# Complex-decay attention with an MLP on one core: weight loads without gates, the log's clip as a job of its own, rstd on two engines, and another order of all jobs

## Chip, cores and metric

The kernel runs on one core of a Trainium2 chip. The metric is the time of one execution on the device in microseconds (us); a lower one is better. The kernel before takes 197.36 us, the median of three runs (196.34 to 197.73). All times are of the fast state unless a run says otherwise.

## The reference, cut to what matters

```python
# q, k, v, a_re, a_im: (4, 8, 768, 48) float32
mag = np.sqrt(a_re**2 + a_im**2)
scale = np.minimum(mag, 0.999) / (mag + 1e-06)      # a complex decay, clipped to 0.999
for t in range(768):                                # S_re, S_im: 48 x 48 for each head
    S_re, S_im = ar*S_re - ai*S_im + k_t v_t^T,  ar*S_im + ai*S_re
    y[t] = q_t @ S_re
x = y with heads side by side                       # (4, 768, 384)
xn = (x - mean) / sqrt(var + 1e-6) * g_ln
out = x + relu(xn @ w_ch1) @ w_ch2                  # 384 -> 1536 -> 384
```

The kernel computes the recurrence in blocks of 128 steps ("tiles", 24 of them), two to a "pair" (12 pairs). For each pair the logarithm and the angle of the decay are summed along time by matmuls, queries and keys are scaled by exponentials and rotated by cosines and sines, and the tile becomes a masked product. The MLP follows per pair.

## The kernel before: the parts that matter here

Every piece of work is a named job, and a long string gives the order of all jobs. Each engine runs its own jobs **strictly in that order**; the letter behind the name is the engine (P TensorE, A ScalarE, V VectorE, G GpSimd, S the loading queue), the digit a PSUM bank.

```python
GATES = (("k", 0, 1), ("aim", 1, 0))
PLAN = """
are.0.1:S tab.log.0:A ln.0.1:A iv.0.1:A aim.0.1:S ... gate.1:G q.0.0:S q.0.1:S warm.0:P1 warm.1:P1
... gate.0:G tab.trig.0:A ... r.2.0:G ... G.0:V1
atm.1:V6 atm.0:V2 y.1:P0 y.0:P6 ... x.0:A6 l.2.0:V dec.2.0:P2 wl.1:G
..."""
```

The weight loads are issued by GpSimd, each behind a tiny copy (the "gate") that waits for an input, so that they don't start before it has landed:

```python
for i, (nm, P, c) in enumerate(GATES):
    g.add(f"gate.{i}", ... nc.gpsimd.tensor_copy(out=probe, in_=...), needs=[f"{nm}.{P}.{c}"], ...)
g.add("wl.0", lambda: nc.gpsimd.dma_start(out=w1b, ...), needs=["gate.0"])
g.add("wl.1", lambda: nc.gpsimd.dma_start(out=w2b, ...), needs=["gate.1"])
```

The log of the decay and its clip are one job of two VectorE instructions:

```python
def f_l(S_=S_):
    nc.vector.scalar_tensor_tensor(out=S_("l"), in0=S_("r2"), scalar=0.5, in1=S_("w"), ...)   # the log
    nc.vector.tensor_scalar(out=S_("l"), in0=S_("l"), scalar1=LNCAP, scalar2=LNEPS,
                            op0=ALU.min, op1=ALU.add)                                        # the clip
```

Jobs named below: `r` is the product of imaginary part and inverse, `ke` and `qe` scale keys and queries, `ks` and `qs` rotate them, `kT`/`ksT` and `qT`/`qsT` are their transposes and the copies out of PSUM, `am`/`atm` the tile's product and its masking, `y` the tile's result, `dec` the matmuls that sum the clipped log, `e` and `en` the exponentials, `wp`/`wc` the folding of the layer norm into w1, `ot` the output's last sum, `bn` and `rstd` the layer norm's statistics, and `warm` a matmul without a result that is meant to keep TensorE's clock up.

Of the kernel before, what the change touches and what calls it, by code (L numbers as in the profile page):

```python
# [33 lines left out]
GATES = (("k", 0, 1), ("aim", 1, 0))  # L34
# [5 lines left out]
are.0.1:S tab.log.0:A ln.0.1:A iv.0.1:A aim.0.1:S are.0.0:S pad.ks.1:G one:G ue:G car0.1:G cmean:G pick:G  # L40
ident:G uth:V zdec:G r.0.1:G aim.0.0:S are.1.0:S ln.0.0:A iv.0.0:A r.0.0:V gln:S aim.1.0:S k.0.0:S are.3.0:S
k.0.1:S r2.0.1:A u.0.1:A pad.ks.2:G l.0.1:V ln.1.0:A r2.0.0:G gate.1:G q.0.0:S q.0.1:S warm.0:P1 warm.1:P1
warm.2:P1 warm.3:P1 warm.4:P1 warm.5:P1 warm.6:P1 warm.7:P1 warm.8:P1 warm.9:P1 warm.10:P1 warm.11:P1
warm.12:P1 warm.13:P1 warm.14:P1 warm.15:P1 warm.16:P1 warm.17:P1 warm.18:P1 warm.19:P1 warm.20:P1
warm.21:P1 warm.22:P1 warm.23:P1 warm.24:P1 warm.25:P1 warm.26:P1 warm.27:P1 warm.28:P1 warm.29:P1
warm.30:P1 warm.31:P1 warm.32:P1 warm.33:P1 dec.0.1:P0 u.0.0:A iv.1.0:A l.0.0:V r.1.0:V car0.0:G en.0.1:A0
e.0.1:A0 q.1.0:S r2.1.0:V pad.qs.0:G gate.0:G tab.trig.0:A th.0.1:A warm.34:P2 warm.35:P2 warm.36:P2
warm.37:P2 warm.38:P2 warm.39:P2 warm.40:P2 warm.41:P2 warm.42:P2 warm.43:P2 warm.44:P2 warm.45:P2
warm.46:P2 warm.47:P2 warm.48:P2 warm.49:P2 warm.50:P2 warm.51:P2 warm.52:P2 ph.0.1:P1 are.2.0:S vf.0.0:S
vf.0.1:S aim.2.0:S th.0.0:A ph.0.0:P0 ke.0.1.0:G abs.0.0:V0 abs.0.1:A1 car.0.1:A1 pad.ks.0:G sin.0.1:A1  # L50
ks.0.1.1:V car.0.0:V0 th.1.0:A warm.53:P4 warm.54:P4 warm.55:P4 warm.56:P4 warm.57:P4 warm.58:P4 warm.59:P4
warm.60:P4 warm.61:P4 ph.1.0:P2 k.1.1:S qe.0.1.0:V cos.0.1:A qs.0.1.0:V cos.0.0:A dec.0.0:P1 sin.0.0:A0
aim.3.0:S vf.1.1:S k.1.0:S abs.1.0:V2 car.1.0:V2 vf.1.0:S q.1.1:S ks.0.1.0:G pad.qs.1:G mask:G tab.log.1:A
en.0.0:A1 e.0.0:A1 qs.0.1.1:V ke.0.0.0:V qe.0.0.0:V ks.0.0.0:V ks.0.0.1:V warm.62:P5 warm.63:P5 warm.64:P5
warm.65:P5 warm.66:P5 warm.67:P5 warm.68:P5 warm.69:P5 warm.70:P5 warm.71:P5 warm.72:P5 warm.73:P5
warm.74:P5 warm.75:P5 warm.76:P5 warm.77:P5 warm.78:P5 warm.79:P5 warm.80:P5 warm.81:P5 warm.82:P5 kT.1:P4
k.2.0:S wl.0:G qs.0.0.1:V u.1.0:A ln.2.0:A qs.0.0.0:V dps.0:P5 k.2.1:S iv.2.0:A l.1.0:V kT.0:P6 qT.1:P7
tab.trig.1:A cos.1.0:A v.0:A ksT.0:V6 r.2.0:G ksT.1:V4 decc.0:V5 wgc:V qsT.1:V7 qT.0:P0 gm.0:P1 dec.1.0:P4
am.1:P6 th.2.0:A sin.1.0:A2 tab.log.2:A e.1.0:A4 r2.2.0:G u.2.0:A pad.qs.2:G qsT.0:V0 am.0:P2 G.0:V1
atm.1:V6 atm.0:V2 y.1:P0 y.0:P6 ln.3.0:A iv.3.0:A wp.2:P7 qe.1.0.0:G x.0:A6 l.2.0:V dec.2.0:P2 wl.1:G  # L60
en.1.0:A4 wp.0:P6 e.2.0:A2 x.1:A0 wc.2.0:V7 wc.2.2:V7 en.2.0:A2 are.4.0:S xtr.0:P0 wc.2.1:V7 dps.1:P7
xtr.1:P4 r.3.0:G xT.0:A0 wp.1:P5 decc.1:A7 ph.2.0:P2 wc.0.0:V6 wc.0.1:V6 bn.0:V wc.0.2:V6 r2.3.0:A xT.1:A4
wc.1.2:V5 wc.1.1:V5 wc.1.0:V5 ke.1.0.0:G ke.1.0.1:G ks.1.0.0:G v.1:G qe.1.0.1:G mm1.0.2.1:P6 gm.1:P1 G.1:V1
mm1.0.2.0:P6 relu.0.2:V6 u.3.0:A aim.4.0:S ks.1.0.1:V qs.1.0.1:V qs.1.0.0:V bn.1:V rstd.0:G abs.2.0:A2
tab.trig.2:A th.3.0:A cos.2.0:A mm1.0.0.1:P4 mm1.0.1.1:P0 mm1.0.0.0:P4 relu.0.0:V4 sin.2.0:A2 k.3.0:S
q.2.1:S mm1.0.1.0:P0 ph.3.0:P6 l.3.0:V relu.0.1:A0 kT.3:P2 gm.2:P3 vf.2.0:S q.2.0:S k.3.1:S kT.2:P0 qT.2:P1
ksT.2:V0 qsT.2:V1 mm2.0.0:P4 mm2.0.1:P4 mm2.0.2:P4 sin.3.0:A6 am.2:P0 abs.3.0:A6 G.2:A3 ksT.3:A2 ke.2.0.0:G
gm.3:P3 qT.3:P5 ke.2.0.1:V ks.2.0.0:V tab.log.3:A ln.4.0:A iv.4.0:A ks.2.0.1:G r.4.0:G atm.2:V0 mm2.1.0:P2
mm2.1.1:P2 qsT.3:V5 vf.2.1:S aim.6.0:S am.3:P0 mm2.1.2:P2 car.3.0:A6 G.3:V3 q.3.1:S q.4.1:S ot.0:V4 kT.5:P3
atm.3:V0 tab.trig.3:A th.4.0:A qe.2.0.1:G qe.2.0.0:G y.2:P5 q.3.0:S are.6.0:S vf.3.1:S st.0:S y.3:P4 x.2:A5  # L70
x.3:A4 kT.4:P6 xtr.2:P7 ot.1:V2 bn.2:V xT.2:V7 xtr.3:P2 xT.3:V2 ksT.4:V6 dec.3.0:P0 mm1.1.0.1:P4
mm1.1.0.0:P4 r2.4.0:A mm1.1.1.1:P6 qs.2.0.1:V qs.2.0.0:V qT.5:P2 mm1.1.1.0:P6 ksT.5:V3 bn.3:V qT.4:P3
tab.log.4:A en.3.0:A0 v.2:A e.3.0:A0 relu.1.1:A6 ph.4.0:P0 relu.1.0:V4 vf.3.0:S gm.4:P4 ke.3.0.1:G qsT.4:V3
am.4:P6 qsT.5:V2 mm2.2.0:P5 am.5:P2 mm2.2.1:P5 tab.trig.4:A cos.3.0:A G.4:A4 rstd.1:G ke.3.0.0:G qe.3.0.1:G
are.5.0:S aim.5.0:S abs.4.0:V0 sin.4.0:A0 car.4.0:A0 atm.4:V6 mm1.1.2.0:P6 dps.3:P4 mm1.1.2.1:P6 tab.log.5:A
u.4.0:A atm.5:V2 qe.3.0.0:G ks.3.0.1:G ks.3.0.0:V qs.3.0.1:V relu.1.2:V6 qs.3.0.0:V y.5:P0 y.4:P1 l.4.0:V
mm2.3.0:P2 x.5:A0 kT.7:P3 mm2.3.1:P2 x.4:A1 xtr.4:P0 mm2.2.2:P5 xtr.5:P1 ln.5.0:A k.4.0:S iv.5.0:A decc.3:A4
ln.6.0:A q.4.0:S k.5.1:S v.3:G ksT.7:V3 dec.4.0:P6 xT.5:V1 xT.4:A0 mm2.3.2:P2 e.4.0:A6 en.4.0:A6 iv.6.0:A
bn.4:V mm1.2.1.1:P0 ot.2:V5 r.5.0:G qsT.7:S r.6.0:G r2.5.0:V mm1.2.1.0:P0 gm.6:P3 qe.4.0.1:V bn.5:V rstd.2:G
ke.4.0.0:G relu.2.1:A0 u.5.0:A mm1.2.0.1:P4 mm1.2.0.0:P4 tab.trig.5:A th.5.0:A mm1.2.2.1:P6 qe.4.0.0:G  # L80
am.7:P0 mm1.2.2.0:P6 ot.3:V2 qsT.6:S ksT.6:S k.5.0:S vf.4.1:S th.6.0:A relu.2.2:A6 vf.4.0:S st.2:S cos.4.0:A
G.6:V3 k.4.1:S q.5.1:S st.1:S gm.7:P3 dps.4:P2 relu.2.0:V4 mm2.5.0:P4 atm.7:V0 l.5.0:V am.6:P0 atm.6:V0
are.8.0:S y.7:P5 mm2.5.1:P4 q.5.0:S ph.5.0:P6 aim.7.0:S mm2.4.0:P0 y.6:P1 x.7:A5 xtr.7:P5 mm2.5.2:P4
r2.6.0:V bn.7:V ke.4.0.1:G v.4:V x.6:V1 xtr.6:P1 sin.5.0:A6 abs.5.0:A6 xT.7:A5 cos.5.0:A decc.4:A2
mm2.4.1:P0 mm2.4.2:P0 are.7.0:S k.6.1:S G.7:V3 ot.5:V4 tab.log.6:A u.6.0:A xT.6:V1 qs.4.0.0:V mm1.3.0.0:P6
dec.5.0:P4 ks.4.0.1:V mm1.3.1.1:P2 ks.4.0.0:V gm.8:P1 mm1.3.0.1:P6 mm1.3.1.0:P2 qs.4.0.1:V ot.4:V0 e.5.0:A4
qe.5.0.0:G kT.9:P0 en.5.0:A4 relu.3.0:A6 kT.8:P4 st.4:S l.6.0:V ln.8.0:A ksT.8:A4 G.8:A1 bn.6:V st.3:S
k.6.0:S qsT.9:S relu.3.1:V2 qe.5.0.1:V qs.5.0.0:V rstd.3:G q.6.1:S aim.8.0:S st.5:S mm1.3.2.0:P6 qT.8:P5
mm1.3.2.1:P6 ln.7.0:A gm.9:P1 relu.3.2:A6 vf.5.0:S mm2.7.0:P4 dec.6.0:P2 qs.5.0.1:G qsT.8:V5 mm2.7.1:P4
iv.7.0:A G.9:V1 ksT.9:V0 ke.5.0.0:V en.6.0:A2 am.8:P6 e.6.0:A2 r.7.0:V vf.5.1:S ph.6.0:P0 mm2.7.2:P4  # L90
qT.10:P5 am.9:P2 vf.6.1:S r2.7.0:A iv.8.0:A ke.5.0.1:V atm.8:V6 ks.5.0.0:G ks.5.0.1:G u.7.0:A y.8:P6 x.8:A6
tab.trig.6:A sin.6.0:A0 r.8.0:G ke.6.0.0:G qT.11:P7 qsT.10:V5 atm.9:V2 qsT.11:V7 mm2.6.0:P5 mm2.6.1:P5
y.9:P6 abs.6.0:A0 car.6.0:A0 kT.10:P7 bn.8:V x.9:V6 ksT.10:V7 xtr.8:P2 kT.11:P3 xtr.9:P6 mm2.6.2:P5 xT.9:A6
xT.8:V2 ksT.11:V3 am.10:P0 vf.6.0:S th.7.0:A mm1.4.1.0:P6 am.11:P2 th.8.0:A ke.6.0.1:G v.5:G mm1.4.1.1:P6
ot.6:V5 oa.7:A4 k.8.1:S are.9.0:S mm1.4.0.0:P4 mm1.4.0.1:P4 atm.10:V0 gm.10:P0 relu.4.1:A6 l.7.0:V
ks.6.0.1:V ph.7.0:P6 y.10:P1 cos.6.0:A atm.11:V2 G.10:V0 y.11:P0 relu.4.0:A4 mm2.9.0:P2 mm1.4.2.1:P4 x.10:V1
x.11:V0 r2.8.0:A mm1.4.2.0:P4 mm2.8.0:P3 dec.7.0:P0 mm2.8.1:P3 mm2.9.1:P2 ks.6.0.0:G car.7.0:A6 sin.7.0:A6
tab.log.7:A ln.9.0:A q.6.0:S q.8.0:S bn.9:V bn.10:V abs.7.0:A6 e.7.0:A0 qe.6.0.1:G qe.6.0.0:G rstd.4:G
ot.7:G v.6:G relu.4.2:V4 mm2.8.2:P3 xtr.10:P4 bn.11:V qs.6.0.0:V en.7.0:A0 qs.6.0.1:V gm.12:P5 dps.6:P6
# [102 lines left out]
def kernel(  # L202
# [60 lines left out]
    def eng(name):  # L263
        return g.ops[name].eng
# [506 lines left out]
```

## Time and profile before

| | before |
|---|---|
| median time, span of the profiled run | 197.36 us, 196.2 us |
| busy: TensorE, VectorE, ScalarE, GpSimd | 178.8, 160.1, 164.1, 107.8 us |
| first matmul of w1 begins at | 39.68 us |
| its TensorE jobs ahead, so *lost in the start* | 11.5 us, 28.2 us |
| *holes* from there to the last matmul | 6.7 us |
| *end*, from the last matmul on | 3.7 us |
| TensorE's granted clock at half, up to the first w1 matmul | 13.7 us |
| full-size logs and clips over their shortest times (0.95 and 0.355 us), in all | 1.1 + 6.7 us |

The three losses in italics, with some 157.7 us of useful matmuls, make the span; the prediction shows how they are worked out. They come from one profiled execution of each kernel, here one of 198.14 us, 0.8 us above the median; differences of about 1 us between two such traces are not firm. The two stretches around the start, with the columns that the prediction explains (length, busy PE, PEld, DVE, ACT, POOL with counts, granted clock, DMA share, GB/s), show what the start costs:

```profile
20.00:30.00 10.00, 6.45 (x92) 5.17 (x92) 9.76 (x19) 9.88 (x12) 5.71 (x5) 0.78 1.03 207
30.00:40.00 10.00, 8.51 (x54) 4.15 (x53) 9.02 (x14) 6.22 (x13) 6.81 (x5) 0.54 1.19 180
```

The clock falls to 0.78 and 0.54 of full, so the busy time of TensorE there is partly half-speed work. The VectorE timeline of pair 2 and the GpSimd timeline of the same moments (start us, length us, engine, line, operation, tiles) show the slow clip:

```profile
30.27 0.95 DVE L449 SCALAR_TENSOR_TENSOR l<-r,w 128x768 f16<-128x768 f16 x1
31.25 1.85 DVE L451 TENSOR_SCALAR l<-l 128x768 f16<-128x768 f16 x1
```

```profile
30.36 2.52 POOL L280 TENSOR_TENSOR r<-aim,are 128x768 f16<-128x768 f32 x1 [0.50 <-ACT are L433]
```

The clip that takes 0.36 us alone got through only when GpSimd's product ended (at 32.88 us). The log before it, begun just ahead of the product, took its 0.95 us.

### The profile page before, as it was taken

The page shows a single profiled execution, that of the slowest core. Times are in us where ns is not written, and L with a number is a line of the kernel's source. Part 1 is how long each engine was busy: PE and PEld are TensorE (multiplying, and loading weights), DVE is VectorE, ACT ScalarE, POOL GpSimd, SP SyncE. Part 2 cuts the span into 40 slices and gives each one's busy share as a digit, 9 for nine tenths or more (in the row PEclk, how much of TensorE's full clock was granted, in tenths as well). Part 3 has the DMA queues.
Part 4 walks back from the last instruction along what each step waited for, and adds up shares of the span by engine and source line. Part 5 has one row for each costly group of instructions (what it writes and reads, how often), then busy time and mean ns, then how long its engine had stood idle before and what let it go on. Part 6 is the DMA issues. An engine that isn't in the chain of part 4 may idle for free.

```text
span 196.2 us, 5114 instructions
## 1 busy us (share of the span) xinstructions
PE 178.8 (91%) x2031; PEld 135.7 (69%) x2032; DVE 160.1 (82%) x268; ACT 164.1 (84%) x226; POOL 107.8 (55%) x127
## 2 busy tenths in 40 slices
PE   4987566999999999999999997999999999998992
PEld 3775443486787777587887785787877868776771
DVE  1449999899999999999998799799969969935702
ACT  4799994989899999999999999897979998565160
POOL 8535558515839359135968699315891376530230
PEclk9999965599999999999999999999999999999999
DMA  5999999999899399899799999999998999994222
GB/s 138 250 220 233 170 233 173 184 242 217 187 250 222 70 172 245 226 230 238 148 226 205 223 163 280 188 212 253 184 222 155 156 203 147 238 197 130 104 84 82
DMA packets 132936, 37.76 MB, mean 192 GB/s; under 512 B 127920, under 2 KB 132528, under 8 KB 132912
## 3 DMA queue, kind: packets, MB, share of 16 engines
q1 hardware_dynamic: 130960, 35.07, 85.3%
q0 software_dynamic: 1952, 2.36, 7.4%
q8 instruction: 16, 0.26, 0.5%
q14 instruction: 8, 0.07, 0.1%
HBM read 28.31 MB, written 4.72 MB: 168 GB/s over the span
## 4 chain that ended last, share of the span: by engine, by line
PE 50%; DVE 20%; ACT 10%; DMA 8%; SPq 5%; issue 4%; POOL 2%; DVEq 0%; POOLq 0%
PE banks L705 16%; PE banks L684 15%; DVE atm L280 5%; DMA are<-in_a_re_dram 4%; SPq L566 3%; PE banks L584 3%; DVE l L449 3%; PE banks L459 3%; DVE h L697 2%; DVE l L451 2%; PE banks L561 2%; DMA q<-in_q_dram 2%; DMA out_dram<-ot 2%; ACT L739 2%; PE banks L655 2%
## 5 line engine op out<-in xcount | busy, mean ns | idle before, releaser
L705 PE MATMUL banks<-w2b,h 128*128 128x384 bf16 x288 | 55.5, 326 | 1.2 <-DVE atm L280 1.1
L684 PE MATMUL banks<-xT,w1b 128*128 128x256 bf16 x432 | 52.2, 272 | 0.4 <-ACT xT L275 0.4
L684 PEld LDWEIGHTS <-w1b 128*128 128x128 bf16 x432 | 41.3, 98 | 7.0 <-issue 1.0
L705 PEld LDWEIGHTS <-h 128*128 128x128 bf16 x288 | 26.2, 98 | 14.9 <-issue 1.6
L280 DVE TENSOR_TENSOR atm<-banks,mask 128x1024 bf16<-128x1024 f32 x24 | 28.9, 1217 | 4.1 <-PE banks L584 4.0
L695 ACT ACTIVATE h<-banks 128x1024 bf16<-128x1024 f32 x27 | 27.0, 1022 | 5.2 <-PE banks L684 5.0
L739 ACT ACT_TABLE_LOAD x20 | 25.7, 1283 | 1.1 <-PEq L755 0.8
L280 POOL TENSOR_TENSOR qe<-q,e 128x384 bf16<-128x384 f32 x16 | 15.8, 996 | 17.3 <-ACT e L463 12.4
L280 POOL TENSOR_TENSOR ks<-ke,trig 128x768 bf16<-128x768 bf16 (+1 forms) x11 | 17.9, 1634 | 12.0 <-DVE ke L280 7.4
L280 POOL TENSOR_TENSOR r<-aim,are 128x768 f16<-128x768 f32 (+1 forms) x9 | 16.5, 1836 | 11.0 <-ACT are L433 11.0
L280 POOL TENSOR_TENSOR ke<-k,en 128x384 bf16<-128x384 f32 x17 | 17.2, 1017 | 8.1 <-ACT en L463 8.1
L719 DVE SCALAR_TENSOR_TENSOR ot<-banks,rstd,x 128x384 f32<-128x384 f32 x20 | 12.0, 610 | 8.7 <-PE banks L705 6.0
L584 PE MATMUL banks<-qsT,ksT 128*128 128x128 bf16 x192 | 15.3, 227 | 1.2 <-DVE qsT L277 1.2
L584 PEld LDWEIGHTS <-ksT 128*128 128x128 bf16 x192 | 12.9, 102 | 3.9 <-issue 2.3
L734 PE MATMUL banks<-u_e 128*128 128x256 f16 x83 | 12.5, 318 | 2.8 <-POOL u_e L312 2.8
L634 PE MATMUL banks<-v,atm 128*128 128x48 bf16 x192 | 12.2, 186 | 1.5 <-DVE atm L280 1.4
L449 DVE SCALAR_TENSOR_TENSOR l<-r,w 128x768 f16<-128x768 f16 (+1 forms) x13 | 12.9, 990 | 0.9 <-ACT r L445 0.8
L634 PEld LDWEIGHTS <-atm 128*128 128x128 bf16 x192 | 10.8, 97 | 3.7 <-DVE atm L280 2.8
L647 DVE BATCH_NORM_STATS2 stats<-x 128x6 f32<-128x384 bf16 x24 | 13.2, 548 | 0.3 <-ACT x L275 0.3
L280 DVE TENSOR_TENSOR qs<-qe,trig 128x768 bf16<-128x768 bf16 (+1 forms) x21 | 12.1, 597 | 1.1 <-POOL qe L280 0.8
L734 PEld LDWEIGHTS <-u_e 128*128 128x128 f16 x83 | 9.4, 113 | 5.0 <-POOL u_e L312 2.4
L477 PE MATMUL banks<-th,u_th 128*128 128x384 f16 (+1 forms) x52 | 12.1, 320 | 0.7 <-ACT th L467 0.7
(91 smaller groups left out, 376.1 us busy)
## 6 DMA issues: line engine op xcount, KB each, us to landing
k<-in_k_dram SPq DMA_DIRECT2D x24, 192.0 KB, 4.2
q<-in_q_dram SPq DMA_DIRECT2D x24, 192.0 KB, 4.1
vf<-in_v_dram SPq DMA_DIRECT2D x24, 192.0 KB, 4.3
out_dram<-ot SPq DMA_DIRECT2D x24, 192.0 KB, 3.2
are<-in_a_re_dram SPq DMA_DIRECT2D x11, 384.0 KB, 4.7
aim<-in_a_im_dram SPq DMA_DIRECT2D x11, 384.0 KB, 5.5
w1b<-in_moe_w_ch_dram POOLq DMA_DIRECT2D x1, 1152.0 KB, 10.1
w2b<-in_moe_w_ch_dram POOLq DMA_DIRECT2D x1, 1152.0 KB, 11.8
```

The costliest lines, as they stand in the source:

```text
L280: {"DVE": nc.vector, "POOL": nc.gpsimd}[eng(name)].tensor_tensor(**kw)
L449: nc.vector.scalar_tensor_tensor(out=S_("l"), in0=S_("r2"), scalar=0.5, in1=S_("w"), op0=ALU.mult, op1=ALU.add)
L477: nc.tensor.matmul(heads(ps[:, c]), lhsT=u_th[:, c, j], rhs=step(T("th", P), j), start=False, stop=(j == R - 1))
L584: nc.tensor.matmul(ps[:, h], lhsT=T("ksT", n)[:, h], rhs=T("qsT", n)[:, h], start=True, stop=True)
L634: nc.tensor.matmul(ps[:, h], lhsT=T("atm", n)[:, h], rhs=T("v", P)[:, c, h], start=True, stop=nfirst)
L647: nc.vector.bn_stats(out=T("stats", n), in_=T("x", n))
L684: nc.tensor.matmul(ps[:, jj], lhsT=w1b[:, dc, ts(gi * JG + jj, C)], rhs=T("xT", P)[:, dc].rearrange("p c t -> p (c t)"), start=(dc == 0), ...
L695: act(out=dst, in_=src, func=AF.Relu)
L705: nc.tensor.matmul(bank(f"o.{n}")[:, 0:DM], lhsT=T("h", P)[:, j, ts(c, C)], rhs=w2b[:, j], start=(j == 0), stop=(j == NJ - 1))
L719: nc.vector.scalar_tensor_tensor(out=T("ot", n), in0=bank(f"o.{n}")[:, 0:DM], scalar=T("rstd", P)[:, ds(c, 1)], in1=T("x", n), op0=ALU.mul ...
L734: g.add(f"warm.{i}", lambda i=i: nc.tensor.matmul(bank(f"warm.{i}")[:, 0:256], lhsT=u_e[:, 0, 0], rhs=u_e[:, 1].rearrange("p j t -> p (j t ...
L739: g.add(f"tab.{nm}.{i}", lambda tab=tab: nc.scalar.preload_act_table_set(tab))
```

## The change

The intent is to drop the two gates and issue the weights later, to let the clip be placed away from the log (and from GpSimd work), to take rstd off GpSimd, and to use an order that was searched anew with these freedoms.

```diff
-GATES = (("k", 0, 1), ("aim", 1, 0))
...
-    probe = pool.tile([C, 1], FP32, name="probe")
+    eps_b = pool.tile([C, 1], FP32, name="eps_b")
...
-    for i, (nm, P, c) in enumerate(GATES):
-        g.add(f"gate.{i}", ...)
-    g.add("wl.0", ..., needs=["gate.0"])
+    g.add("wl.0", ...)
-    g.add("wl.1", ..., needs=["gate.1"])
+    g.add("wl.1", ...)
...
-                nc.vector.tensor_scalar(out=S_("l"), in0=S_("l"), scalar1=LNCAP, scalar2=LNEPS,
-                                        op0=ALU.min, op1=ALU.add)
             add(f"l.{X}", f_l, needs=[f"u.{X}"], ...)
+            add(f"lc.{X}", lambda S_=S_: nc.vector.tensor_scalar(out=S_("l"), in0=S_("l"), ...),
+                needs=[f"l.{X}"], uses=[("l", P)])
...
-            add(f"dec.{X}", f_dec, needs=[f"l.{X}", "ue"], ...)
+            add(f"dec.{X}", f_dec, needs=[f"lc.{X}", "ue"], ...)
...
         def f_rstd():
+            if eng(f"rstd.{P}") == "ACT":
+                act(out=t, in_=T("mv", P)[:, :, 1], func=AF.Ln, bias=eps_b)
+                act(out=t, in_=t, func=AF.Exp, scale=-0.5)
+                return
...                                    (the whole PLAN is another one; of its start:)
+... l.2.0:V am.1:P6 car.1.0:A4 ... atm.1:V6 y.1:P6 warm.92:P7 warm.93:P7 ... wl.0:G qe.1.0.1:G qe.1.0.0:G
```

The number of warm-up matmuls in the new order is 107 instead of 83.

## The prediction

> **What bounds the kernel now.** I read the page's busy shares first, then the slices, the TensorE groups, the chain in order of time, the clip's instructions, and the per-engine timelines of the first 45 us. From the page (busy us, then the 40 slices of 4.9 us each):
>
> ```profile
> PE 178.8 (91%) x2031; PEld 135.7 (69%) x2032; DVE 160.1 (82%) x268; ACT 164.1 (84%) x226; POOL 107.8 (55%) x127
> ...
> PEclk9999965599999999999999999999999999999999
> DMA  5999999999899399899799999999998999994222
> ...
> L705 PE MATMUL banks<-w2b,h 128*128 128x384 bf16 x288 | 55.5, 326 | 1.2 <-DVE atm L280 1.1
> L684 PE MATMUL banks<-xT,w1b 128*128 128x256 bf16 x432 | 52.2, 272 | 0.4 <-ACT xT L275 0.4
> ```
>
> The reader is to see three engines above 80% and a halved TensorE clock early on. Matmuls overlap, so I don't take PE's 91% as work. In the chain and the timeline a full run of matmuls shows the real spacing:
>
> ```profile
> 138.97 3.93 PE banks L684 x36
> ...
> 188.64 3.91 PE banks L705 x24
> 192.58 0.62 DVE ot L719
> ```
>
> 36 matmuls in 3.93 us are 0.109 us each, 24 in 3.91 us are 0.163 each. So 432 x 0.109 + 288 x 0.163 = 94 us. The other TensorE jobs, by the same reading of the timeline, are: attention products 24 x 0.45, y 24 x 0.40, ks and qs transposes 23 x 0.45, x transposes 22 x 0.17, decay sums 12 x 0.65, phases 12 x 0.98, state updates 5.3, end decays 2.3 and the weight sums 2. Altogether about **157.7 us of useful TensorE work** at full clock (the 83 warm-up matmuls are not in it). The span is 196.2, so 38.5 us are not used, in three places:
> - *start*: the first matmul of w1 begins at 39.68 us. The jobs ahead of it in the order come to 11.5 us, so 28.2 us are lost there.
> - *middle*: from 39.7 to the last matmul at 192.6 is 152.9 us for 146.2 us of work: 6.7 us of small holes.
> - *end*: 3.6 us from the last matmul to the end.
>
> The stretches of 40 us show that the middle has no slack on three engines (columns: stretch, length, PE, PEld, DVE, ACT, POOL busy with counts, granted clock, DMA share, GB/s):
>
> ```profile
> 40.00:80.00 40.00, 38.41 (x486) 29.92 (x484) 38.91 (x62) 38.98 (x51) 24.24 (x23) 1.00 0.92 201
> 80.00:120.00 40.00, 39.72 (x489) 31.14 (x486) 37.68 (x65) 39.21 (x55) 26.19 (x24) 1.00 0.97 212
> ```
>
> One hole is the subject of the change. The chain around 117 us (start, us, what):
>
> ```profile
> 117.10 1.41 DVE l L449
> 118.57 1.57 issue
> 120.14 1.22 DVE atm L280
> 121.40 2.11 PE banks L705 x12
> ```
>
> The "issue" is the clip (the log's second VectorE instruction), which took 1.68 us there; TensorE waited 1.2 us for the masked product behind it.
>
> **What the Trainium skill says.**
> - *SBUF — State Buffer*, "Who interferes with whom": VectorE and GpSimd share a port pair as an exclusive lock; a one-input VectorE instruction in a two-port mode waits for a whole GpSimd instruction. The trace agrees: the 768-element clip took 0.36 us the four times GpSimd was idle, and 0.95 to 1.86 us the seven times one ran beside it.
> - *ScalarE: Activation LUTs*, "What ACT_TABLE_LOAD costs": 1283 ns for the load and about 1380 ns of drain. The trace shows the 1283 (20 loads, 25.7 us) but no drain: a load at 10.75 us is followed by an activation at 12.04.
> - *TensorE: Matmul & The Clock Gate*, "What's actually happening": the clock halves after an idle window. The trace agrees: mean granted clock 0.78 at 20 to 30 us and 0.54 at 30 to 40, after VectorE kept TensorE waiting.
> - *DMA: Bandwidth & Descriptors*, "Queues, rings and completion order": an engine goes round between queues packet by packet. So weights should slow the loads beside them; each weight transfer took 10.1 and 11.8 us here, with the DMA share near 1.
>
> **The change part by part** (counts from the two plans, durations from the groups by form).
> 1. *Gates removed.* Two GpSimd copies of 0.18 us go, with waits of 2.5 and 0.6 us in the first 13 us. The weights now stand later in GpSimd's order: w1 goes behind r of pair 3, whose input I expect about 21 us (loads landed in order at about 221 GB/s before), so issue near 23.5 instead of 17.8, landing near 34 instead of 28. Its use stands later too, so I count 0.
> 2. *Clip apart.* The count stays at 13; it may now stand away from the log and from GpSimd work. The seven slow clips cost (2 x 1.5 + 1.3 + 4 x 0.6) = 6.7 us over 0.36. In most pairs the clip still directly follows the log. I give it 2 to 3 us of VectorE time, perhaps 1 to 1.5 us of TensorE holes.
> 3. *rstd on two engines.* Ten of twelve go from GpSimd (0.71 + 0.23 us each, 9.4 us; its first instruction is behind 17.2 us of GpSimd waiting) to two tiny activations, about 0.2 us each by the 0.16 us of the smallest copy: ScalarE + 4.
> 4. *Order and placement.* ScalarE: five more table loads +6.4, seven more scaled copies of the output +4.1, three fewer relus -3.1, v, x, xT, G, car and the rest about -2. With rstd **+9 us, to 173**. VectorE: four more r +3.8, three relus +3.6, r2, G, car, ke, abs and qsT +7.6, against -6 qe, -6 qs, -7 ot, -7 xT and smaller ones -15: **0**. GpSimd: +6 qs, +6 qe, +7 ot against -4 r, -10 rstd: **+5, to 113**. TensorE: +2 qT, -1 kT, -4 xtr are -0.2 us; 24 more warm-ups stand in idle time. DMA: three more transposes of about 1.3 us of queue. So no engine has less to do; only the order can pay.
> 5. *Start.* In the new order the jobs ahead of the first w1 matmul are 16.5 us, 5 more than before (pair 1's transposes, products and phase come first). By hand, with the durations of the old timeline: r of the first half at 8 us, phase about 15, exps 17.7 (9.9 before), third log table about 24 (25.7 before), then ScalarE's own work in order up to the xT copy at 44.5. VectorE has 38 us of work ahead of that point, beginning at 7.5, which comes to 42 to 46. So the first w1 matmul comes about 45.5, the start loses 45.5 - 16.5 = 29.0 us: **0.8 worse**. But pairs 1 to 3 are further ahead on ScalarE and VectorE by then.
> 6. *Middle.* The holes fall from 6.7 to about 3.5, by the head start, the clip and the new order: **-3.2**. This is a choice, not a sum: holes can't gain more than 6.7, and ScalarE has 9 us more to place.
> 7. *End.* Both orders end with 36 and 24 dense matmuls, an output and a store: **0**.
>
> Sum: 29.0 + 157.5 + 3.5 + 3.6 = 193.6 us of span, and +1.2 for the gap between span and the median of runs: **194.8 us**.
>
> **Rivals.**
> - *ScalarE becomes the bound.* For it: 39 of 40 us busy in both middle stretches and 9 us more work. Its 173 us plus about 6 idle at the start and 8 to 10 at the end is 187 to 189: below 193.6, but any stall is then not made up. If it binds, holes grow to 8 and the time is 199.
> - *The start decides, and well.* Before, the clock was half for some 10 us; the new warm-ups stand among the early jobs. If VectorE and ScalarE reach xT at 42 instead of 45.5, the span falls to 190. Against it: 38 us of VectorE work ahead of that point.
> - *The later weights bind.* If GpSimd reaches w1's issue at 28 rather than 23.5, landing is near 39, and the weight sums and nine rescalings (0.74 us each on VectorE) push the start to 49: time 198. Or they only move contention from early loads to those of pairs 3 and 4.
> - *GpSimd's extra 12 qs and qe hold VectorE up* by the lock, giving back the clip's gain: 197, the same.
>
> **Range and chances.** The terms not fixed by a count are the start (3 us either way) and the holes (1 to 8 us): 190.5 to 199 us. 2% is below 193.4, which needs both a start no worse than before and holes of 3 us or less; an order that was searched for and kept speaks a little for it: 0.37. Slower than 201.3 needs a start of 3 us worse and holes of 8: 0.09. The rest is within 2%.
>
> **What would show it.** First w1 matmul near 45 us with the clock high before it (step 5); w1's landing before the weight sums want it (1); clips with a median nearer 0.4 us and no chain piece like that at 118.57 (2); ScalarE busy 171 to 175 and 25 table loads (3, 4); fewer than 4 us of holes from there to the last matmul (6). The prediction is wrong if the start moves by more than 4 us, or if ScalarE or the queue of transposes makes a hole of several us that I can't see in the order.

## The result

The changed kernel gives correct results and takes **204.03 us** (median of 4 runs, 203.39 to 204.91), the kernel before 197.29 us in the same rounds. The ratio is **1.035** with a 95% interval of 1.030 to 1.041: slower. A ratio here is the mean time of one kernel's fast runs over that of the other's of the same rounds, so not quite the ratio of the two medians. All runs were fast.

| | before | after | predicted |
|---|---|---|---|
| span | 196.2 | 202.3 | 193.6 |
| first w1 matmul at | 39.68 | 49.51 | 45.5 |
| lost in the start | 28.2 | 33.0 | 29.0 |
| holes | 6.7 | 7.7 | 3.5 |
| end | 3.7 | 4.1 | 3.6 |
| ScalarE, VectorE, GpSimd busy | 164.1, 160.1, 107.8 | 172.6, 159.2, 109.1 | 173, 160, 113 |
| TensorE's clock at half, up to the first w1 matmul | 13.7 | 6.8 | "high" |
| full-size logs + clips over their shortest times | 1.1 + 6.7 | 3.9 + 2.1 | (none given) + about 4 |

The page after, in the lines that answer to those of before (busy time; the clock in 40 slices; the chain's shares by engine; the table loads):

```profile
PE 179.5 (89%) x2052; PEld 136.9 (68%) x2052; DVE 159.2 (79%) x264; ACT 172.6 (85%) x247; POOL 109.1 (54%) x119
...
PEclk9999997599999999999999999999999999999997
...
PE 40%; ACT 26%; DVE 19%; issue 5%; DMA 3%; POOL 3%; SPq 2%; DVEq 1%; POOLq 0%; ACTq 0%
...
L747 ACT ACT_TABLE_LOAD x25 | 32.1, 1283 | 1.2 <-PEq L763 0.8
```

The busy times are near the predicted ones and the clock is better than before, and still the kernel is slower. So the time is not in an engine's sum; it is in who waits for whom. The stretches after:

```profile
20.00:30.00 10.00, 7.16 (x113) 5.38 (x110) 8.67 (x18) 9.89 (x14) 5.42 (x5) 1.00 0.99 203
30.00:40.00 10.00, 6.13 (x43) 4.11 (x44) 9.96 (x15) 6.55 (x10) 1.85 (x3) 0.66 1.12 247
40.00:50.00 10.00, 9.56 (x119) 6.80 (x118) 8.40 (x14) 9.95 (x12) 7.82 (x9) 1.00 1.06 198
```

Between 30 and 40 us VectorE is full while TensorE falls to 43 matmuls and ScalarE to 6.55 us. The chain of waits in order of time says what VectorE did (start, length, what):

```profile
7.08 6.81 PE banks L742 x37
...
14.90 1.75 PE banks L742 x16
...
28.35 0.47 DVE r L284
28.83 3.85 DVE l L452
32.67 1.15 DVE atm L284
33.87 0.22 PE banks L638
```

37 warm-ups take 6.81 us and 16 more 1.75 us, on the chain; and one log (L452) takes 3.85 us on it. The timelines of VectorE and GpSimd for these moments:

```profile
28.27 0.56 DVE L284 TENSOR_TENSOR r<-r 128x768 f16<-128x768 f16 x1
28.75 3.93 DVE L452 SCALAR_TENSOR_TENSOR l<-r,w 128x768 f16<-128x768 f16 x1
32.60 1.21 DVE L284 TENSOR_TENSOR atm<-banks,mask 128x1024 bf16<-128x1024 f32 x1
```

```profile
28.17 1.00 POOL L350 DMA_DIRECT2D w1b<-in_moe_w_ch_dram  x1
29.20 1.79 POOL L284 TENSOR_TENSOR qe<-q,e 128x384 bf16<-128x384 f32 x2
30.94 0.91 POOL L284 TENSOR_TENSOR ke<-k,en 128x384 bf16<-128x384 f32 x1
```

The log got through only behind the whole row on GpSimd, that is w1's issue, two query products and a key product: the row ends at 31.85 us and the log 0.8 us later, 3 us late. Behind it stands the masked product of tile 1, behind that TensorE's `y.1`, and behind that, since every engine is in order, the phase of pair 2 and then ScalarE's cosines and sines. The TensorE and ScalarE timelines (in brackets the idle time before, and what ended it):

```profile
33.87 0.22 PE L638 MATMUL banks<-v,atm 128*128 128x48 bf16 x1 [4.52 <-DVE atm L284]
...
49.51 1.47 PE L692 MATMUL banks<-xT,w1b 128*128 128x256 bf16 x12
```

```profile
17.01 0.49 ACT L467 ACTIVATE e<-banks 128x384 bf16<-128x384 f32 x1 [2.12 <-PE banks L463]
...
37.07 0.81 ACT L506 ACTIVATE trig<-banks 128x768 bf16<-128x768 int16 x1 [3.37 <-PE banks L481]
```

Up to there ScalarE had been on the predicted track (exponentials at 17.0 for a predicted 17.7); it then stood for 3.37 us.

### The profile page after: what moved, and what is told of

Its sections match the earlier page's. It is cut to its first block, busy times and chain, and to the rows that moved or that the text cites. A ratio compares the mean times of both kernels' runs of the same rounds, so it can differ in the third digit from the quotient of the medians.

```text
span 202.3 us, 5166 instructions
## 1 busy us (share of the span) xinstructions
PE 179.5 (89%) x2052; PEld 136.9 (68%) x2052; DVE 159.2 (79%) x264; ACT 172.6 (85%) x247; POOL 109.1 (54%) x119
## 4 chain that ended last, share of the span: by engine, by line
PE 40%; ACT 26%; DVE 19%; issue 5%; DMA 3%; POOL 3%; SPq 2%; DVEq 1%; POOLq 0%; ACTq 0%
PE banks L692 12%; PE banks L713 10%; PE banks L742 5%; ACT L747 5%; DVE l L452 4%; PE banks L481 3%; ACT e L467 2%; ACT en L467 2%; PE banks L588 2%; ACT h L703 2%; ACT r L448 2%; DMA q<-in_q_dram 2%; DVE atm L284 2%; ACT trig L506 2%; DVE r L284 2%
## 5 line engine op out<-in xcount | busy, mean ns | idle before, releaser
L284 POOL TENSOR_TENSOR qe<-q,e 128x384 bf16<-128x384 f32 x22 | 21.4, 979 | 30.4 <-ACT e L467 16.4
L713 PEld LDWEIGHTS <-h 128*128 128x128 bf16 x288 | 26.1, 97 | 15.8 <-DVE h L705 1.2
L747 ACT ACT_TABLE_LOAD x25 | 32.1, 1283 | 1.2 <-PEq L763 0.8
L703 ACT ACTIVATE h<-banks 128x1024 bf16<-128x1024 f32 x24 | 24.3, 1023 | 4.7 <-PE banks L692 4.7
L284 POOL TENSOR_TENSOR ks<-ke,trig 128x768 bf16<-128x768 bf16 x12 | 19.8, 1660 | 9.7 <-DVE ke L284 9.1
L742 PE MATMUL banks<-u_e 128*128 128x256 f16 x107 | 16.8, 319 | 7.1 <-POOL u_e L317 7.1
L705 DVE TENSOR_SCALAR h<-banks 128x1024 bf16<-128x1024 f32 x12 | 14.6, 1220 | 8.1 <-PE banks L692 8.0
L725 POOL TENSOR_TENSOR ot<-ot,x 128x384 f32<-128x384 f32 x11 | 10.1, 925 | 17.2 <-ACT ot L718 17.2
L284 POOL TENSOR_TENSOR qs<-qe,trig 128x768 bf16<-128x768 bf16 (+1 forms) x11 | 17.4, 1585 | 3.2 <-ACT trig L509 3.0
L284 POOL TENSOR_TENSOR ke<-k,en 128x384 bf16<-128x384 f32 x14 | 14.2, 1012 | 8.3 <-PE banks L616 6.6
L452 DVE SCALAR_TENSOR_TENSOR l<-r,w 128x768 f16<-128x768 f16 (+1 forms) x13 | 15.4, 1187 | 2.1 <-ACT r L448 2.0
L284 POOL TENSOR_TENSOR r<-aim,are 128x768 f16<-128x768 f32 x5 | 9.3, 1866 | 9.2 <-ACT are L436 5.3
L284 DVE TENSOR_TENSOR r<-aim,are 128x768 f16<-128x768 f32 (+1 forms) x8 | 8.0, 1002 | 7.2 <-ACT are L436 7.2
```

The lines of the kernel that those rows point to most:

```text
L284: {"DVE": nc.vector, "POOL": nc.gpsimd}[eng(name)].tensor_tensor(**kw)
L703: act(out=dst, in_=src, func=AF.Relu)
L705: nc.vector.tensor_scalar(out=dst, in0=src, scalar1=0.0, scalar2=None, op0=ALU.max)
L713: nc.tensor.matmul(bank(f"o.{n}")[:, 0:DM], lhsT=T("h", P)[:, j, ts(c, C)], rhs=w2b[:, j], start=(j == 0), stop=(j == NJ - 1))
L725: nc.gpsimd.tensor_tensor(out=T("ot", n), in0=T("ot", n), in1=T("x", n), op=ALU.add)
L742: g.add(f"warm.{i}", lambda i=i: nc.tensor.matmul(bank(f"warm.{i}")[:, 0:256], lhsT=u_e[:, 0, 0], rhs=u_e[:, 1].rearrange("p j t -> p (j t ...
```

## The experiments

Seventeen more kernels ran. Each gave correct results. Ratios are to the kernel before in the same rounds. "Gates off, old order" below is the old order run by the new code: no gates, every clip right behind its log, the old places of everything else.

### 1. The log of pair 2 out of the way

```diff
-... l.2.0:V am.1:P6 ... atm.1:V6 ... qsT.0:V2 G.1:V1 ksT.0:V3 ...
+... am.1:P6 ... atm.1:V6 ... qsT.0:V2 G.1:V1 ksT.0:V3 l.2.0:V ...
```

> The changed kernel with one VectorE instruction moved: the log sum of pair 2 stands behind the copies of chunk 0 instead of in front of the masked product of chunk 1. In the changed kernel it took 3.93 us (0.95 elsewhere) beside w1's issue and three GpSimd products, and everything up to the first w1 matmul came some 3 us late. Theory (that lock-out is most of the loss at the start): 201.0 us, 3 less than the changed kernel's 204.0; first w1 matmul near 46.5 us. Rival (the extra ScalarE work, or late weights): no gain, 203.5 to 204.5.

Measured: 201.05 us, ratio 1.019 (1.015 to 1.024). One job moved by a few places gave back 3.0 of the 6.7 us. The first w1 matmul came at 46.05 instead of 49.51 us, near the predicted 45.5. Its VectorE timeline has both logs of pairs 2 and 3 in one entry of two, after the GpSimd row is over:

```profile
31.60 1.81 DVE L452 SCALAR_TENSOR_TENSOR l<-r,w 128x768 f16<-128x768 f16 x2
```

So 0.9 us each. That one job's place is shown as the largest single part of the loss. The 3.5 us at the start hold two things that this run doesn't part: the wait itself, and the slower clock behind it. TensorE's clock stood at half for 6.8 us after its wait of 4.52 us in the changed kernel, and for 3.4 us here.

### 2. What kept the log out: w1's issue or the products

The other way to unlock it is to leave the log where it is and move the weights. Both loads were put earlier in the changed kernel, so that w1's issue no longer leads the row:

```diff
-... v.0:G ... r.3.0:G ... wl.0:G qe.1.0.1:G ...        wl.1:G where it stood
+... wl.0:G v.0:G ... r.3.0:G wl.1:G ... qe.1.0.1:G ...
```

> The changed kernel with w1's load issued about 5 us earlier (in front of v of pair 0 in GpSimd's order, near where it was before the change), w2's behind r of pair 3. The log of pair 2 keeps its place. If w1's issue itself holds VectorE out, the log takes some 1 us less and the time is 203. If the row of GpSimd products holds it out, the log still takes 3 to 4 us and the time is 203.5 to 204.5. If late weights cost the time, 201 or less.

Measured: 201.98 us, ratio 1.024 (1.019 to 1.029). This lies between the outcomes that were expected for a log of normal length and for late weights. w2's issue now stood where w1's had, but it was over (at 28.68 us) before the log began, and the log came in between the two query products:

```profile
28.96 1.66 DVE L452 SCALAR_TENSOR_TENSOR l<-r,w 128x768 f16<-128x768 f16 x1
```

It took 1.66 us instead of 3.93 beside the same two query products, so 2.3 us of the 3.0 went with the moved issue, and the first w1 matmul came 2.1 us earlier (47.44 us). The two products took 2.68 us this time (1.79 before): GpSimd did part of the waiting. Whether w1's issue itself held the lock, or only shifted the products against the log, stays open, for the traces disagree. For a shift: `r2` of pair 3, the square of `r`, is a VectorE product with both inputs in SBUF too; in the changed kernel it ran wholly inside w1's issue (from 28.27 us) and took 0.56 us, as elsewhere; and the log at 29.80 us in experiment 7 began inside w2's issue and took 0.95 us. For a hold: in this run `r2` took 1.30 us beside w2's issue, and in the changed kernel the log was held although it began 0.45 us before the first product.

### 3. Fewer warm-up matmuls

```diff
 (on top of experiment 1)
-warm.12:P1 ... warm.36:P1      (25 of 37 ahead of the first phase)
-warm.41:P3 ... warm.52:P3      (12 of 16 ahead of the first decay sum)
```

> The previous kernel (log of pair 2 later) with fewer warm-up matmuls early: 12 of 37 before the first phase, 4 of 16 before the first decay sum. They took 6.4 and 1.7 us; the phase's input was ready at 9.6 and the decay's at 13.4 us, so ScalarE stood idle 1.6 us for its first exp. Theory (warm-ups stand in the way of real jobs): ScalarE's chain and the first w1 matmul come 1.5 us earlier (near 44.5), 199.5 us. Rival (that idle time returns as other waits, or the clock falls): 201 or more.

Measured: 199.44 us, ratio 1.011 (1.007 to 1.016), 0.8% of the whole; the first w1 matmul came at 44.71 us. The TensorE timeline, first of the changed kernel, then of this one:

```profile
7.08 6.81 PE L742 MATMUL banks<-u_e 128*128 128x256 f16 x37 [7.08 <-POOL u_e L317]
13.73 0.25 PE L478 MATMUL banks<-car,pick 96*128 96x192 f16 x1
```

```profile
7.07 2.72 PE L738 MATMUL banks<-u_e 128*128 128x256 f16 x12 [7.07 <-POOL u_e L313]
9.58 0.37 PE L474 MATMUL banks<-car,pick 96*128 96x192 f16 x1
```

With 12 warm-ups the first phase is not at full speed yet (0.37 us a matmul instead of 0.25), but it begins 4.15 us earlier, and that is worth more. The granted clock later was no worse: at half for 3.4 us before the first w1 matmul, as in experiment 1 (13.7 before).

### 4. rstd back to GpSimd

```diff
 (on top of experiment 1)
-rstd.P:A       (ten of them)
+rstd.P:G       (at the same places)
```

> The kernel with the log of pair 2 later, and all twelve rstd on GpSimd instead of two. It takes 10 x 0.48 = 4.8 us from ScalarE, which is 99% busy from 70 to 130 us. Theory that ScalarE's added work costs the rest: 199 us or less (2 less than 201.05). Rival (the start alone): 200.5 to 201.5.

Measured: 203.45 us, ratio 1.030, against 1.019 without it. That the two activations of rstd on ScalarE cost the time (the theory in the expectation) is wrong: in this order rstd is better there. The rest of ScalarE's extra work is not tested by this. The holes rose to 11.7 us, with logs and clips locked out more: 3.5 + 2.0 us over their shortest times, against 0.8 + 2.1 in experiment 1.

### 5. The gates alone

```diff
 the order before, in the code after:
-gate.0:G  gate.1:G
-l.P:V
+l.P:V lc.P:V
```

> The order of the kernel before in the changed code: the gates gone, clip directly behind the log as before, rstd on GpSimd, weights at the same place in GpSimd's order. Theory: 197.3 us, 0 +- 1, as the gates' waits of 2.5 and 0.6 us were not on the chain. Rival (without gates the loads of the start are slowed): 199 or more.

Measured: 197.29 us, ratio 0.999 (0.995 to 1.003). Gates off with the old order is worth nothing, as step 1 had it. This kernel is the base of the four kernels of experiment 7.

### 6. Splices of the two orders

```diff
 x_bstart:  the order before up to the first w1 matmul, then what is left of the order after
 x_astart:  the order after up to there, then what is left of the order before
```

> The order of the kernel before up to its first w1 matmul, then everything else in the changed order (clip apart, rstd on ScalarE, five more table loads in all but the start). Theory (the start lost 4.8 of the 6.1 us): 198.5 us, within 1.5 of the kernel before. Rival (the rest of the order with 8 us more ScalarE work costs the time): 202 or more.

> The changed order up to its first w1 matmul, then everything else in the order of the kernel before. Theory (start): 202 to 204 us, first w1 matmul near 49.5 us. Rival (rest of the order): 197 to 199.

Measured: 209.42 us (ratio 1.061) and 217.39 us (ratio 1.100), both worse than either whole. The seams had holes of 1 to 2.7 us of their own, and the first w1 matmul came only at 55.8 and 55.6 us; presumably the second half's order assumes the first half's state. These two say nothing on which half is at fault; they are misses.

### 7. The new parts, one by one, in the old order

First the clip, moved away from the log in six pairs:

```diff
 (on top of gates off, old order)
-l.P:V lc.P:V ...                for P in 1, 3, 5, 6, 8, 10
+l.P:V ... lc.P:V                (a later place on VectorE, still ahead of dec.P)
```

> The order of the kernel before without gates, with six clips moved one to four VectorE instructions behind their log, to where GpSimd was idle or TensorE does not wait. The slow clips cost 5.2 us of VectorE over the 0.36 us of a free one. Theory (clip apart, alone, pays): 195.0 us, with no hole of 1.2 us before w2's matmuls near 121 us. Rival (VectorE's freed time is off the chain): 197.3.

Measured: 196.43 us, ratio 0.996 (0.991 to 1.000), the same, and short of the 195.0 expected. In the trace the holes did fall, from 6.8 to 4.6 us. But the clip of pair 1 had moved into a longer lock-out (2.11 us), and the log of pair 2 then met GpSimd's product:

```profile
30.49 2.59 DVE L448 SCALAR_TENSOR_TENSOR l<-r,w 128x768 f16<-128x768 f16 x1
33.12 0.95 DVE L451 TENSOR_SCALAR l<-l 128x768 f16<-128x768 f16 x1
```

Start lost 1.9 us, holes gained 2.2. Here a clip moved alone traded one lock-out for another.

Next, the GpSimd work that is in the way, moved to VectorE:

```diff
 (on top of gates off, old order)
+lc.3 behind qsT.2, lc.5 behind x.6, lc.6 behind bn.6, lc.8 behind abs.9, lc.10 behind ot.13
-r.2.0:G  r.3.0:G
+lc.1.0:V r.2.0:V ... lc.2.0:V r.3.0:V
```

> The order of the kernel before, without gates, with five clips moved to where GpSimd is idle (pairs 3, 5, 6, 8, 10; pair 1's stays behind its log, where moving it met a longer lock-out), and r of pairs 2 and 3 made by VectorE right behind the clip, instead of by GpSimd beside it (2.2 us there, with the clip held to 1.86). The first two clips should take 0.36 us, r 0.95 each. Theory (the lock-outs set the time of the start and the holes): 195.0 us, 1% under the kernel before; holes 4.6 us or less, first w1 matmul at 38 us. Rival (VectorE's own work of 1.9 us more eats it): 196.5 to 197.5.

Measured, in five rounds: **193.24 us, ratio 0.978 (0.974 to 0.982)**, better than both kernels, and better than expected. The five clips and the two products moved together; beside the run above, with six clips moved and no product (196.43 us), the products are the larger part, but no run moved them alone. GpSimd no longer has a product to run while VectorE does the log and the clip, and VectorE pays 0.95 us for the product:

```profile
29.80 0.95 DVE L448 SCALAR_TENSOR_TENSOR l<-r,w 128x768 f16<-128x768 f16 x1
30.78 0.36 DVE L451 TENSOR_SCALAR l<-l 128x768 f16<-128x768 f16 x1
31.06 0.95 DVE L280 TENSOR_TENSOR r<-aim,are 128x768 f16<-128x768 f32 x1
```

Full-size logs and clips over their shortest times came to 1.7 + 0.5 us, from 1.1 + 6.7. The first w1 matmul is at 36.92 us, the holes are 5.2.

Third, rstd on ScalarE in the old order, at the next place with the log table:

```diff
 (on top of gates off, old order)
-rstd.P:G       for P in 0 to 4, 6, 7, 8
+rstd.P:A       (inside a stretch with the log table loaded)
```

> The order of the kernel before without gates, with eight of the twelve rstd on ScalarE (those with the log table in place), two small activations each, 0.48 us. If that part alone costs by ScalarE's load: 198.5 or more. If it frees VectorE from lock-outs: 196 or less. Theory (off the chain): 197.3 +- 0.8.

Measured: 204.09 us, ratio 1.034 (1.030 to 1.039). This is a miss of my theory: I had counted the activations (0.28 + 0.20 us each) and not the wait. ScalarE came to pair 0's rstd before the statistics were there, and stood; ScalarE's waits (who waited for what, then us in total, times, longest):

```profile
ACT rstd L671 <- DVE mv L648: 5.1, 1, 5.1
```

In the changed kernel the same activations never waited. A job of an in-order engine costs what its inputs make it wait, and that belongs to the order, not to the job.

Fourth, the later w1 alone:

```diff
 (on top of gates off, old order)
-wl.0:G where it stood
+... r2.2.0:V wl.0:G ...        (some 8 us later)
```

> The order of the kernel before without gates, with w1's load issued 7 us later (behind the square of r of pair 2, near 24.6 us instead of 17.3). It would land near 35, its first use was at 30.5. Theory (late weights must come with a later place for their use, as the changed order had): first w1 matmul 4 us later, 200 to 202 us. Rival (early loads gain by it): 197 or less.

Measured: 201.67 us, ratio 1.021 (1.017 to 1.025). The first w1 matmul moved from 38.1 to 42.8 us. The load landed at 36.2 us and TensorE waited 4.68 us for it, for this order first needs w1, in its weight sums, at about 30.2 us. The changed kernel's first weight sum stands at 43.6 us, and there w1 landed at 38.4 and was not waited for.

### 8. The holes behind the start

Experiment 3's kernel is still 1.1% slower than before, by its holes (8.1 us). A first try was to take two small jobs of the first MLP out of ScalarE's way:

```diff
 (on top of experiment 3)
+decc.3 ahead of ksT.3,  relu.0.0 ahead of ln.5.0
```

> The kernel with the log later and fewer warm-ups (199.4 us), with the end decay copy of pair 1 and the first relu each a few ScalarE instructions earlier: TensorE waited 0.6 us for the one and 0.7 for the other near 47 us. Theory (holes of the first w1 and w2 groups are the rest of the loss): 198.2 us. Rival (ScalarE's order only hands the wait on): 199 to 200.

Measured: 200.19 us, ratio 1.013. No gain: TensorE now waited 1.81 us at 49.0 us for another copy of ScalarE. A second try took up VectorE's logs and clips at 55 to 59 us, which again stood beside a row on GpSimd. Before that, in experiment 3's VectorE timeline:

```profile
55.54 1.58 DVE L448 SCALAR_TENSOR_TENSOR l<-r,w 128x768 f16<-128x768 f16 x1
57.16 0.95 DVE L451 TENSOR_SCALAR l<-l 128x768 f16<-128x768 f16 x1
58.03 1.67 DVE L448 SCALAR_TENSOR_TENSOR l<-r,w 128x768 f16<-128x768 f16 x1
```

```diff
 (on top of experiment 3)
-ke.3.0.0:G ot.0:G ...
+... ke.3.0.0:V ks.3.0.1:V ... qs.3.0.0:G ot.0:G
```

> The run with later log and fewer warm-ups (199.4 us, ratio 1.0114), with GpSimd's add of output tile 0 put behind its row of products of pair 3 and GpSimd's last key product of pair 3 given to VectorE right before its rotation. Theory (the last 2 us against the kernel before are logs and clips of pairs 4 and 5 that VectorE runs at 1.58, 0.95 and 1.67 us beside a row of four GpSimd instructions at 55.4 to 58.9 us): two of the four are gone, the three take about 2.7 us instead of 4.2, VectorE pays 0.5 us for the product, the two holes of TensorE at 63 and 64 us shrink from 1.6 to about 0.7, the time is 198.4 and the ratio 1.006. Rival (the holes at 63 and 64 us are what this order leaves whatever VectorE does, because the copies wait for TensorE's transposes and those for the chain of pair 3): 199.3 to 199.8, ratio 1.010 to 1.014.

Measured, in five rounds: 199.1 us, ratio 1.007 (1.003 to 1.011). The same three instructions afterwards:

```profile
55.68 0.96 DVE L448 SCALAR_TENSOR_TENSOR l<-r,w 128x768 f16<-128x768 f16 x1
56.67 0.36 DVE L451 TENSOR_SCALAR l<-l 128x768 f16<-128x768 f16 x1
56.95 0.95 DVE L448 SCALAR_TENSOR_TENSOR l<-r,w 128x768 f16<-128x768 f16 x1
```

They took 2.3 us instead of 4.2, and TensorE's waits of 0.59 and 0.65 us at 63 and 64 us are gone; but new ones stand elsewhere, and all holes fell only from 8.1 to 7.6. The ratio is close to what the theory said, but its interval overlaps that of experiment 3, so the last 0.4% are likely, not shown. The remaining 0.7% stay open; no single wait of TensorE behind the start is longer than 0.6 us in this trace.

### 9. What the later weight loads are worth

With the lock-out gone, the weights can be moved without touching it. All four runs start from the last kernel (1.007), where w1 is issued at 26.1 us and w2 at 39.4.

```diff
 e13_both:      wl.0 ahead of v.0,  wl.1 behind r.3.0     (issued at 19.7 and 26.2 us)
 e14_w1early:   wl.0 ahead of v.0                         (19.6 and 39.6)
 e15_w2early:   wl.1 behind r.3.0, by mistake AHEAD of wl.0   (27.5 and 26.2)
 e16_w2behind:  wl.1 right behind wl.0                    (26.1 and 27.1)
```

> The same with w1's load issued before GpSimd's values cast of tile 0 and w2's load behind the real part of pair 3, about 6 and 17 us earlier (as in the earlier run with early w1). Theory (with the log of pair 2 out of the row, the late w1 costs nothing more: it landed 0.3 us before its use): same as the run beside it within 0.5 us. Rival (the late loads still hold the scaling of w1 back, and with it the first phase): faster by 0.5 to 1.5 us, mainly in the start.

Measured: 203.37 us, the median of its three fast runs, ratio 1.031 (1.026 to 1.037); 206.29 us with all six. Three of the six, the profiled one among them, are counted as slow, being over 1.5% above its fastest, so its trace shows the kind of wait rather than its size. It is neither what the theory nor what the rival said, and the same move had not hurt in experiment 2. The VectorE timeline and that of the loading queue:

```profile
40.65 0.63 DVE L280 TENSOR_TENSOR ke<-k,en 128x384 bf16<-128x384 f32 x1 [8.82 <-DMA k<-in_k_dram]
```

```profile
21.31 10.66 SPq L386 DMA_DIRECT2D k<-in_k_dram  x2
32.02 4.32 SPq L386 DMA_DIRECT2D vf<-in_v_dram  x1
```

Issuing two key loads took the queue 10.66 us beside the weight transfers (1.73 us in experiment 8's kernel), a key landed 18.6 us after its issue, and VectorE stood for 8.82 us. In experiment 2's fast run with both loads early a key load landed 17.1 us after its issue too, but there the keys were waited for 0.5 us only. Nor do late weights keep the queue free: in experiment 8's kernel issuing two decay rows took it 9.88 us from 28.47 us on. They move the slow stretch to other loads. The next runs tell the two weight loads apart.

> The run with the second lock-out lightened (ratio 1.0071), with w1's load alone moved ahead of GpSimd's values cast of tile 0 (issue at about 19.7 us instead of 26.1); w2's stays late. If the pair of early loads made the 3.1% of the last run by standing in the way of the key loads (the two 1.2 MB transfers then run one behind the other for 25 us, and the key of pair 1 landed 18.6 us after its issue), one of them alone does much less: theory 1.007 to 1.012, keys landing within 9 us. Rival (w1 alone is what blocks): 1.02 or more, first w1 matmul after 48 us.

Measured: 199.71 us, ratio 1.012 (1.006 to 1.017). The keys landed 9.6 us after their issue in the median and 11.5 at most (4.7 and 12.0 in the base; 9 at most was expected), and the first w1 matmul came 1.0 us later, at 45.66. The ratio is as expected, though the interval overlaps that of the base.

> The same with w2's load alone moved behind the real part of pair 3 (issue at about 27.3 us instead of 39.4, right behind w1's). Theory (what hurts is the two weight transfers back to back over the loads of pairs 2 and 3, from 26 to 50 us now instead of 20 to 40): the key and query loads issued at 26 to 40 us come late; ratio 1.01 to 1.03, first w1 matmul at 46 to 50 us. Rival (only w1 early together with w2 early reaches the keys of pair 1): 1.005 to 1.009, unchanged.

Measured: 206.73 us, the median of three fast runs (a fourth, of 210.29 us, counts as slow), ratio 1.049 (1.042 to 1.056). This run had a fault of mine: w2 was put in front of w1 on the same queue, w1 landed 17.3 us after its issue, and TensorE waited for it:

```profile
44.78 1.46 PE L366 MATMUL banks<-w1b,gc 128*128 128x512 bf16 x3 [6.31 <-DMA w1b<-in_moe_w_ch_dram]
```

So it measures mostly a late w1 (4.2% with a landing at 44.8 us instead of 38.0) and can't tell what an early w2 costs. Mended:

> The last run put w2's load in front of w1's by mistake, so that w1 landed behind it and the first phase waited 6.5 us for it. Here w2's load stands right behind w1's, at about 27.2 us instead of 39.4, with everything else as in the run with the second lock-out lightened (ratio 1.0071). Theory (the loads of pairs 2 to 5 that are issued from 27 to 40 us then run beside two weight transfers): ratio 1.012 to 1.025, query and decay-row loads landing 3 to 8 us later, first w1 matmul 46 to 48 us. Rival (w2's transfer only waits its turn behind w1's and takes nothing from the others): 1.005 to 1.009.

Measured: 201.53 us, ratio 1.018 (1.009 to 1.026). A query load issued at 26.9 us landed 17.4 us later, and the GpSimd timeline has a wait of 4 us for it:

```profile
44.43 0.91 POOL L280 TENSOR_TENSOR qe<-q,e 128x384 bf16<-128x384 f32 x1 [4.02 <-DMA q<-in_q_dram]
```

TensorE then had a wait of 2.1 us before 48.3 us, where the base waits 0.4. The start was not touched (44.66 us, where 46 to 48 was expected), the holes rose from 7.6 to 10.4. In this order the later w2 is worth about 1% and the later w1 perhaps 0.5%; both together gave 2.4%. That this is more than the sum is not clear of the noise, and that two transfers one behind the other cover some 20 us of the start is an explanation, not a test.

### The runs in one table

The ratio is of all fast runs; the other columns are of one profiled execution.

| kernel | ratio | first w1 | start lost | holes |
|---|---|---|---|---|
| before | 1 | 39.68 | 28.2 | 6.7 |
| after | 1.035 | 49.51 | 33.0 | 7.7 |
| + later log (1) | 1.019 | 46.05 | 29.5 | 7.5 |
| + fewer warm-ups (3) | 1.011 | 44.71 | 28.2 | 8.1 |
| + GpSimd row lightened (8) | 1.007 | 44.69 | 28.2 | 7.6 |
| gates off, old order (5) | 0.999 | 38.09 | 26.6 | 6.8 |
| gates off, clip away (7) | 0.996 | 40.02 | 28.5 | 4.6 |
| gates off, five clips away, r to VectorE (7) | 0.978 | 36.92 | 25.4 | 5.2 |

## Why the prediction was wrong

It said 194.8 us (190.5 to 199) and gave "slower" a chance of 0.09; the kernel took 204.0. What it named for that case, a bad start and holes of 8 us together, is what came. The busy times were right to 4 us. Step by step:

1. **Gates, later weights: 0.** The gates are 0, as run 5 shows. w1's issue came at 28.17 us instead of 23.5, for GpSimd waited 3.4 us for ScalarE before it, and landed at 38.4 instead of 34. It still did not bind. What the step missed is that the later w2 *helps* the order it stands in (experiment 9), by about 1%; and that w1's issue led the row that locked the log out.
2. **Clip apart: -1 to -1.5 us.** The mechanism is right: 11 of 13 clips ran fast after, and their excess fell from 6.7 to 2.1 us. But the log, with two SBUF inputs, took over: 3.9 us from 1.1, 3.0 of it in one place on the chain. The step priced the clip and not its neighbour. The Trainium skill's page *SBUF — State Buffer*, section "Who interferes with whom", says it: a VectorE instruction with two SBUF inputs contends with a GpSimd instruction that reads SBUF. I used only its other half, on the one-input clip; the traces agree with both (the clip 0.36 us alone and 0.95 to 1.86 beside GpSimd; the log 0.95 alone and 1.58 to 3.93 in the rows shown above).
3. **rstd to ScalarE: +4 us of ScalarE.** 5.0 us for the ten (0.30 + 0.20 us each). It gains in this order (run 4) and costs 3.5% in the old one (run 7).
4. **Busy sums: +9, 0, +5.** (In that step "-6 qe" and the like count jobs, and -15 us is their sum.) ScalarE right to 0.4 us, VectorE to 1, GpSimd 4 less, 25 table loads. "No engine has less to do; only the order can pay" stands.
5. **Start: 45.5 us, 29.0 lost. This step failed.** It was 49.51 and 33.0. The hand count added durations from the old timeline, each at its free value, and had no term for a lock-out of VectorE on the path. With the log moved by one experiment the start is 46.05 and 29.5, within 0.6 us of the prediction. So one term, 3.5 us, was missing: the lock-out and the slower clock behind it. That the rest agrees so closely is in part luck, for step 4 also took the many warm-ups for free ("24 more warm-ups stand in idle time"), and dropping 37 of them gave another 1.3 us.
6. **Holes: 3.5 us. This failed too.** They were 7.7. I had called it a choice, resting on a head start and an order "that was searched for". New lock-outs came at 60 to 64 us (logs of 1.15 and 1.67 us, a clip of 0.95). That the first lock-out spent the head start is not borne out: with the start mended the holes stay at 7.5 to 8.1. Only part of their cause is shown.
7. **End: 0.** 0.4 us more.

In sum: of 202.3 - 193.6 = 8.7 us of span, 4.0 are step 5, 4.2 step 6, 0.5 the end and rounding. What the prediction reads from the clock needs a limit too: it was at half for 13.7 us before, not "some 10", and it fell at about 25.8 us, when no wait of TensorE in the 7 us before had been longer than 1.44 us. So the trace shows the halving, but not that a whole idle window comes first.

Of the rivals, the one that GpSimd's extra qs and qe hold VectorE up by the lock had the mechanism, at 197 us, but I charged it against the clip's gain and not to the start. "The later weights bind" had the right numbers (issue at 28, landing near 39, start at 49; 198 us for the whole) for a wrong reason: no matmul waited for them.

Why the searched order came out worse is only argued. If it was searched with fixed durations, it could not see that a log beside a GpSimd row takes 3.93 us.

## What to carry to other kernels

When VectorE and GpSimd share the work, count for each two-input VectorE instruction on the path what GpSimd runs at that moment, and price the lock-out, not the instruction: here it took an instruction from 0.95 to 3.93 us, and TensorE and ScalarE behind it stood for 4.52 and 3.37 us. Two cures paid: to move the victim (204.0 to 201.1 us in the new order), and to take the GpSimd job beside it over to VectorE (197.3 to 193.2 us in the old one, with five clips moved as well). Later weight loads, another engine for a small job, and a warm-up are each worth something only within an order; test them in the order in which they'll stand.

## What the Trainium skill lacked or had wrong

- *SBUF — State Buffer*, "Who interferes with whom", says of VectorE's two-port modes that the engine that issues first gets the shared ports "for the whole instruction". Here one wait went over more than one: the log of pair 2 took 3.93 us beside w1's issue and three products that GpSimd ran without a gap, and 1.66 us beside two products when the issue had moved. The page has no figure for a row of instructions.
- The same section says that a DMA never contends with a compute engine, and that where one seems to, GpSimd was kept from its ports while it prepared the load. It doesn't say outright what VectorE pays, and infers that preparing a load needs only the write side, which a two-input product doesn't take. The runs agree in most cases (0.56 us for `r2` inside an issue) and disagree in one (1.30 us); with w1's issue of 1.00 us at the head of the row the log took 2.3 us longer. If the issue holds the ports or only shifts the row is open.
- *ScalarE: Activation LUTs*, "What ACT_TABLE_LOAD costs": the load of 1283 ns agrees (25 loads in 32.1 us), but the drain of about 1380 ns that the page names does not show in this trace: 23 of the 25 loads are followed by an activation within 0.02 us.
- *TensorE: Matmul & The Clock Gate*, "What's actually happening", puts the warm-up at about 3.4 us of sustained work. The runs agree in kind: after 2.72 us of warm-ups the phase's matmuls still took 0.37 us, after 6.81 us 0.25. The page doesn't weigh the warm-up against the delay of the job behind it: here dropping 37 of them gained 0.8%.
- *DMA: Bandwidth & Descriptors*, "Queues, rings and completion order", says that an engine goes round its queues packet by packet, with no figure for what a small load then waits. Beside two early weight loads of 1152 KB a key load of 192 KB landed 17.1 us after its issue, and beside w1 and w2 one behind the other a query load 17.4 us, both in fast runs (with both late 12.1 at most, 4.7 in the median for the keys). With w1 alone early, issuing two key loads took that queue 7.27 us instead of 1.73.
